# An attention and SiLU-MLP kernel: a hand-written interleaving exchanged for the order of a list scheduler, with chunked weight loads and 512-byte q and k rows

## The chip, the cores and the metric

One core of one Trainium2 chip runs the whole program. The metric is the device time of one execution in microseconds (us). Five engines work side by side and wait for one another by semaphores: TensorE (PE; its weight loads are listed apart as PEld), VectorE (DVE), ScalarE (ACT), GpSimd (POOL) and SyncE (SP), which here only issues transfers. Each engine executes its own list of instructions strictly in the order in which the program wrote it; an instruction that waits holds up everything behind it on that engine.

## The reference, cut to what matters

Inputs are q, k and v of shape (8 batches, 8 heads, 576 tokens, 64), w_in (512 x 2048) and w_out (2048 x 512), all float32. Per batch and head there are two attentions whose outputs are added:

```python
q_d, k_d, v_d = means over groups of 4 tokens          # 144 x 64 each
out_up    = repeat(softmax(q_d k_d^T / 8) v_d, 4)
mask      = |i - j| < 4
out_local = softmax(where(mask, q k^T / 8, -1e9)) v
x = out_up + out_local             # heads side by side: 4608 x 512
h = x @ w_in
out = (h * sigmoid(h)) @ w_out     # 4608 x 512, float32
```

## The kernel before, in words

**Pairs.** The 64 (batch, head) combinations are worked on as 32 pairs of heads; four pairs make one batch of 576 tokens. A pair p goes through these steps:

- `load(p)` on SP: q (`qs`) and k (`ks`) as [96, 12, 64] float32, that is rows of 64 elements (256 bytes); v twice, in five overlapping windows for each head (`vs`, two transfers, 256-byte rows) and in groups of four tokens (`vq`, 1024-byte rows). The staging tiles have two buffers each.
- `cast(p)` and `castv(p)` on POOL: q and k to bf16 (`qb`, `kb`), v to bf16 (`vb`), and the group sums of v (`vt`, `vd`).
- `ph_T`: TensorE transposes q and k (six 96-column blocks each) and forms their group means by a matmul with a small matrix `G_bf` of 24 columns. DVE copies the q results out of PSUM (`qT`, `qd`), ACT those of k (`kT`, `kd`).
- `ph_S1`, `ph_S2`: the scores of the band and of the small attention; ACT takes exp into `Pt` and `Pd`; DVE multiplies `Pt` by the band mask (`do_mask`).
- `ph_Z(z)`, once for two pairs 2z and 2z+1: row sums by matmuls with ones. ACT copies them to `zc`; then SP sends them through `zr` (40 x 72), DVE takes the reciprocal (`rr`, L387), SP writes it to a DRAM scratch `scr` and four transfers spread it over the partitions as `Rb` (L394).
- `ph_PV`: the products with v; DVE multiplies by `Rb` into `xo` (L417, L419), and `do_add` (L435) adds the small attention's part and writes the pair's 576 columns of `xT`, a ring of XR = 2048 token columns.

All these PSUM results share two double banks, `duo0` and `duo1`, taken in turn.

**MLP.** Tokens are handled in nine supers of 512. A `g1` tile is four matmuls into `hps` (contraction 512, weights `w_in_sb` in float32r), tanh on ACT (L453), and one DVE instruction (L455) that makes `gT`. A `g2` tile is four matmuls into `ops`; after four of them ACT copies the block to `osb` and SP writes it out. Each super has 16 g1 and 16 g2 tiles: 144 of each in all. Super j can start when all pairs of the batches that hold its tokens are in `xT`: `fill` demands 4 * min(j, 7) + 4 finished pairs.

**What sets the order.** `Prog.op` appends each operation to its engine's list and adds the semaphore waits that the data need. The order is that of the calls in the loop over `it`: T of pair it, two MLP tiles, Z, one tile, S1, two tiles, S2, two tiles, the reciprocal chain, PV of pair it - 3, two tiles. The list `mlp` alternates g1 of super j with g2 of super j - 1. Ahead of the loop two pairs are loaded, the constants (identity, `G_bf`, mask) are made on POOL between the first casts, and then POOL issues the loads of all of w_in (one transfer, 4096 KB) and all of w_out (one transfer, 2048 KB as bf16).

## Time and profile before

| | before |
|---|---|
| median of 3 runs (lowest to highest) | 485.42 us (484.01 to 486.57) |
| the profiled execution | 482.44 us |
| its span, first to last instruction | 480.7 us |
| mean granted TensorE clock | 0.954 of full speed |
| PE busy / DVE / ACT / POOL | 374.1 / 208.3 / 201.5 / 150.2 us |
| packets, of which under 512 B | 141718, 120946 |

How the rows further down are read. A row of the timeline has the start in us from the start of the span, the duration in us, the engine (SPq is the issue of a transfer on SP), the line, the operation with its output and inputs, and how many instructions were merged (x8); in square brackets stands how long the engine had been idle just before and what ended that. Two merged matmul groups can overlap on paper, so the price of a group is the distance from its start to the start of the next. A row of busy time by stretch has the stretch, its length, and for PE, PEld, DVE, ACT and POOL the busy us with the number of instructions; then the granted clock, the share of time that the core's transfer engines were busy, and GB/s. A row of a group of instructions has its mean duration in ns and the idle time before it.

### The profile page before, as it was taken

The numbers are of one execution on the slowest core, as the hardware profiler recorded it, in microseconds if no ns is written. First come the engines' busy times: TensorE is split into PE (matmuls) and PEld (weight loads), VectorE is DVE, ScalarE is ACT, GpSimd is POOL, SyncE is SP. The second block draws the span as 40 slices with busy tenths as digits, with TensorE's granted clock in tenths as the row PEclk, the third lists the DMA queues.
The fourth block names the chain that finished last, engine by engine and source line by source line (L and its number), as shares of the span: only waits on it lengthen the run. The fifth ranks groups of instructions, "written<-read, shape, count | busy, mean of one in ns | idle before, by whom it ended". The sixth has DMA issues, their size and how long they took to land.

```text
span 480.7 us, 7698 instructions
## 1 busy us (share of the span) xinstructions
PE 374.1 (78%) x3072; PEld 223.4 (46%) x3072; DVE 208.3 (43%) x361; ACT 201.5 (42%) x357; POOL 150.2 (31%) x187
## 2 busy tenths in 40 slices
PE   2311235299519997999899699979998979999997
PEld 1211223166306554555556365546554535555553
DVE  0210215157514564555666445655554554334320
ACT  3220224056405554556465345545654323444431
POOL 5922452632262424334352534244430000000000
PEclk9999999999658998999999979999998989999999
DMA  9999497692668695959689676969572031011012
GB/s 185 305 281 204 119 202 149 125 210 51 143 124 171 141 225 144 184 136 221 147 176 187 136 164 148 216 135 180 125 153 85 26 130 61 22 45 44 22 45 87
DMA packets 141718, 67.95 MB, mean 141 GB/s; under 512 B 120946, under 2 KB 132210, under 8 KB 141170
## 3 DMA queue, kind: packets, MB, share of 16 engines
q1 hardware_dynamic: 139090, 61.17, 58.7%
q0 software_dynamic: 2592, 6.29, 4.9%
q8 instruction: 24, 0.39, 0.4%
q14 instruction: 12, 0.10, 0.1%
HBM read 59.72 MB, written 9.63 MB: 144 GB/s over the span
## 4 chain that ended last, share of the span: by engine, by line
PE 65%; DMA 14%; SPq 7%; DVE 5%; POOL 4%; issue 3%; ACT 2%; POOLq 0%; ACTq 0%
PE hps L300 29%; PE ops L300 25%; PE duo L300 8%; DMA ks<-in_k_dram 5%; DMA zr<-zc 4%; SPq L381 4%; PE duo L310 3%; DMA vq<-in_v_dram 2%; DVE xT L435 2%; SPq L269 2%; DMA Rb<-scr 1%; DVE xo L417 1%; ACT th L453 1%; DMA scr<-rr 1%; POOL kb L278 1%
## 5 line engine op out<-in xcount | busy, mean ns | idle before, releaser
L300 PE MATMUL hps<-xT,w_in_sb 128*128 128x512 f32 x576 | 188.0, 448 | 37.3 <-DVE xT L435 32.6
L455 DVE SCALAR_TENSOR_TENSOR gT<-th,hps 128x512 bf16<-128x512 f32 x144 | 98.9, 687 | 149.0 <-ACT th L453 148.6
L300 PE MATMUL ops<-w_out_bf,gT 128*128 128x512 bf16 x576 | 151.2, 391 | 0.0
L453 ACT ACTIVATE th<-hps 128x512 f32<-128x512 f32 x144 | 86.0, 597 | 152.9 <-PE hps L300 152.7
L300 PEld LDWEIGHTS hps<-xT,w_in_sb 128*128 128x128 f32 x576 | 108.2, 198 | 74.7 <-DVE xT L435 36.2
L300 PEld LDWEIGHTS ops<-w_out_bf,gT 128*128 128x128 bf16 x576 | 46.7, 99 | 65.9 <-issue 26.1
L278 POOL CAST qb<-qs 96x768 bf16<-96x768 f32 x32 | 26.2, 820 | 126.4 <-DMA qs<-in_q_dram 103.0
L322 ACT ACTIVATE kT<-duo 128x576 bf16<-128x576 bf16 x32 | 20.8, 651 | 57.9 <-PE duo L300 57.9
L286 POOL TENSOR_TENSOR vt<-vq 72x512 f32<-72x512 f32 x32 | 41.1, 1286 | 6.8 <-DMA vq<-in_v_dram 6.6
L335 ACT ACTIVATE Pt<-duo 128x912 bf16<-128x912 f32 x32 | 29.7, 929 | 28.5 <-PE duo L300 28.5
L300 PE MATMUL duo<-qT,kT 64*128 64x112 bf16 (+1 forms) x320 | 20.0, 236 | 25.5 <-DVE qT L317 21.3
L284 POOL CAST vb<-vs 128x640 bf16<-128x640 f32 x32 | 24.0, 750 | 44.4 <-PE duo L300 28.7
L387 DVE RECIPROCAL rr<-zr 40x72 f32<-40x72 f32 x17 | 10.1, 593 | 62.5 <-DMA zr<-zc 62.5
L358 DVE TENSOR_TENSOR Pt<-Pt,mask_bf 128x1152 bf16<-128x1152 bf16 x32 | 25.5, 798 | 25.4 <-ACT Pt L350 18.5
L310 PE MATMUL duo<-id_bf,qb 96*128 96x96 bf16 x192 | 16.5, 233 | 25.5 <-POOL qb L278 25.5
L278 POOL CAST kb<-ks 96x768 bf16<-96x768 f32 x32 | 28.2, 882 | 25.3 <-DMA ks<-in_k_dram 24.7
L300 PEld LDWEIGHTS duo<-qT,kT 64*128 64x128 bf16 x320 | 11.1, 103 | 46.0 <-issue 36.0
L469 ACT ACTIVATE osb<-ops 128x512 f32<-128x512 f32 x36 | 21.5, 598 | 24.4 <-PE ops L300 23.8
L435 DVE TENSOR_TENSOR xT<-xo 128x576 fp32r<-128x576 f32 (+4 forms) x40 | 30.7, 783 | 0.6
L310 PEld LDWEIGHTS duo<-id_bf,qb 96*128 96x128 bf16 x192 | 12.1, 112 | 32.7 <-POOL qb L278 26.3
L288 POOL TENSOR_TENSOR vd<-vt 72x256 bf16<-72x256 f32 x32 | 24.5, 766 | 4.3
L417 DVE TENSOR_TENSOR xo<-duo,Rb 128x456 f32<-128x456 f32 x32 | 19.1, 596 | 7.4 <-DMA Rb<-scr 6.7
(43 smaller groups left out, 245.2 us busy)
## 6 DMA issues: line engine op xcount, KB each, us to landing
Rb<-scr SPq DMA_DIRECT2D x68, 180.0 KB, 3.6
vs<-in_v_dram SPq DMA_DIRECT2D x64, 160.0 KB, 4.7
...
```

The lines of the kernel that those rows point to most:

```text
L278: pool(lambda g, a=a, bb=bb: g.tensor_copy(bb[j][:, :, :, :], a[i][:, :, :].rearrange("p (h c) d -> p c h d", h=2)), r=[R(f"{nm}s{i}")], w ...
L284: pool(lambda g: g.tensor_copy(vb[m][:, :, :], vs[i][:, :, :]), r=[R(f"vs{i}")], w=[R(f"vb{m}")])
L286: pool(lambda g: g.tensor_tensor(vt[:, :, :], vq[i][:, :, 0:128], vq[i][:, :, 128:256], ALU.add), r=[R(f"vq{i}")], w=[R("vt")])
L288: pool(lambda g: g.tensor_tensor(vd[m][:, :, :], vt[:, :, 0:64], vt[:, :, 64:128], ALU.add), r=[R("vt")], w=[R(f"vd{m}")])
L300: return P.op("PE", lambda t: t.matmul(out_, lhsT, rhs, start=start, stop=stop, skip_group_check=True), r, w)
L310: P.op("PE", lambda t, c=c, st=st, tps=tps: t.transpose(tps[:, 96 * c:96 * c + 96], st[j][:, c, :, :].rearrange("p h d -> p (h d)"), id_bf ...
L335: P.op("ACT", lambda e: e.activation(Pt[m][:, :, 0:456], D[:, :, 0:456], AF.Exp, scale=0.125), r=bk, w=[R(f"P{m}")])
L358: P.op("DVE", lambda e: e.tensor_tensor(Pt[m][:, :, :], Pt[m][:, :, :], mask_bf[:, :].unsqueeze(1).to_broadcast([128, 2, S_]), ALU.mult), ...
L417: P.op("DVE", lambda e: e.tensor_tensor(xo[x][:, 0:456], D[:, 0, 0:456], Rb[u][:, 0:456], ALU.mult), r=[bk[0], R(f"Rb{u}")], w=[R(f"xo{x}")])
L435: P.op("DVE", lambda e, dst=dst, in0=in0, in1=in1: e.tensor_tensor(dst, in0, in1, ALU.add), r=[R(f"xo{x}")], w=xblk(kc, t, e_))
L453: P.op("ACT", lambda e: e.activation(th[tb][:, :], hps[hb][:, :], AF.Tanh, scale=0.5), r=[R(f"h{hb}", True)], w=[R(f"th{tb}")])
L455: P.op("DVE", lambda e: e.scalar_tensor_tensor(gT[j % 2][:, f, :], th[tb][:, :], 1.0, hps[hb][:, :], ALU.add, ALU.mult), r=[R(f"h{hb}", Tr ...
```

## The change

1. **Order.** The loop and `fill` go. Each step becomes a task with the tasks it needs, the tiles it reads and writes, and a check of the ring; `Prog` carries a clock for each engine and for the two transfer queues, fed by a table of costs in the code. At each step the scheduler issues whatever side work (loads, casts, masks, reciprocals, spreads of `Rb`) is due, then the attention task that its model says is ready (those of the same TensorE mode first, then PV, Z, S2, S1, T), else a g1 or g2 tile.
2. **Weights** come in eight transfers (`load_w`): w_in in four column chunks, w_out in four row chunks, each issued on POOL behind the loads of pairs 3 to 7.
3. **512-byte rows.** q and k are loaded as [96, 6, 128]: two neighbouring tokens in one row. The transposed blocks come out with even and odd tokens apart, so the copies `qT` (DVE) and `kT` (ACT) now write with a step of two elements; `G_bf` gets 48 columns and its matmuls accumulate in twos.
4. **Direct row sums for pairs 2 and 3** (`ph_ZD`, `do_recipD`): row sums on 64 columns of ones into the MLP's own banks `ops` and `hps`, and the reciprocal by DVE straight from there into `Rb`, in five pieces a pair, with no transfers.
5. **Smaller items.** The casts of q and k of the first four pairs move from POOL to DVE (q) and ACT (k); all constants are made before POOL's first cast of v; `Rb` has 4 buffers instead of 3; the ring `xT` has 1536 columns instead of 2048, and PV of a batch waits in the schedule until the supers that it overwrites have been read; the spread of `Rb` is a task of its own (`do_bcast`).

```diff
-        XR = 2048
+        XR = 1536
-        NST, NVB, NP_, NR = 2, 5, 5, 3
-        qs = sb("qs", [96, 12, 64], F32, NST)
+        NST, NVB, NP_, NR, NEARLY = 2, 5, 5, 4, 4
+        qs = sb("qs", [96, 6, 128], F32, NST)
...
+                    t[i][:, :, :], src[b, h:h + 2].rearrange("h (c p r) d -> p (h c) (r d)", p=96, r=2)),
...
+                src = tps[:, :].rearrange("p (c r g) -> p c r g", c=3, r=2)
+                dst = xt[j][:, :].rearrange("p (c g r) -> p c r g", c=3, r=2)
                 if nm == "q":
-                    P.op("DVE", lambda e, tps=tps: e.tensor_copy(qT[j][:, :], tps[:, :]),
+                    P.op("DVE", lambda e, src=src, dst=dst: e.tensor_copy(dst, src),
...
+        def load_w(c):
+            if c < 4:
+                P.op("POOL", lambda g: g.dma_start(
+                    w_in_sb[:, :, 512 * c:512 * c + 512],
...
-        P.op("POOL", lambda g: g.dma_start(w_in_sb[:, :, :], moe_w_in.rearrange("(kc p) f -> p kc f", p=128)),
-        for it in range(NPAIR + LAG):
-            if it < NPAIR:
-                ph_T(it)
...
+        wsteps = {3: (0, 1), 4: (2, 3), 5: (4,), 6: (5, 6), 7: (7,)}
+        before = {4: 'w1', 5: 'w3', 6: 'w4', 7: 'w6'}
...
+            task(attn, f"PV{p}", "PE", [f"rD{p}_4" if p in direct else f"b{z}", f"cv{p}"] +
+                 ([f"Z{z}"] if p not in direct else []) + [nm("PV", p - 1)],
+                 [R(f"P{m}"), R(f"Pd{m}"), R(f"vb{n}"), R(f"vd{n}"), R(f"Rb{u}")], duo_w,
+                 lambda p=p: ph_PV(p), "col", lambda p=p: ring_ok(p))
...
+            if ready:
+                ready.sort(key=lambda c: (c[2][6] != mode[0], c[1]))
...
+            elif mready:
+                if len(mready) == 2:
+                    want = "g2" if (last not in ("g1", "g2") or last == "g1") else "g1"
```

**Place 1: SP, around the first spread of `Rb`.** Before, from the loads of pair 4 on (`zr`, `scr` and `Rb` belong to pairs 0 and 1):

```order
L262 DMA qs<-in_q_dram 96x12x64
L262 DMA ks<-in_k_dram 96x12x64
L269 DMA vs<-in_v_dram 128x5x64 x2
L271 DMA vq<-in_v_dram 72x4x256
L381 DMA zr<-zc 10x1x72 x4
L388 DMA scr<-rr 40x72
L394 DMA Rb<-scr 64x720 x4
L262 DMA qs<-in_q_dram 96x12x64
```

Now, from the q load of pair 5 on, up to the same `Rb` (the `zr` transfers stand ahead of pair 4's loads):

```order
L291 DMA qs<-in_q_dram 96x6x128
L291 DMA ks<-in_k_dram 96x6x128
L445 DMA scr<-rr 40x72
L302 DMA vs<-in_v_dram 128x5x64 x2
L304 DMA vq<-in_v_dram 72x4x256
L291 DMA qs<-in_q_dram 96x6x128
L291 DMA ks<-in_k_dram 96x6x128
L302 DMA vs<-in_v_dram 128x5x64 x2
L304 DMA vq<-in_v_dram 72x4x256
L454 DMA Rb<-scr 64x720 x4
```

The first `Rb` stood behind the loads of five pairs and now stands behind those of seven.

**Place 2: PE, where a batch's last PV meets the next super.** Before, the end of pair 11, and the first g1 tile of super 2 right behind it:

```order
L300 MATMUL duo<-qT,kT 128x120 x2
L300 MATMUL duo<-qd,kd 72x144 x4
L300 MATMUL ops<-w_out_bf,gT 128x512 x4
L300 MATMUL duo<-Pt,vb 64x120 x2
L300 MATMUL duo<-Pt,vb 64x112 x6
L300 MATMUL duo<-Pt,vb 64x120 x2
L300 MATMUL duo<-Pd,vd 64x144 x4
L300 MATMUL hps<-xT,w_in_sb 128x512 x4
```

Now, the PV of pairs 18 and 19 (pair 19 is the last that super 4 needs):

```order
L347 MATMUL duo<-Pt,vb 64x120 x2
L347 MATMUL duo<-Pt,vb 64x112 x6
L347 MATMUL duo<-Pt,vb 64x120 x2
L347 MATMUL duo<-Pd,vd 64x144 x4
L347 MATMUL duo<-Pt,vb 64x120 x2
L347 MATMUL duo<-Pt,vb 64x112 x6
L347 MATMUL duo<-Pt,vb 64x120 x2
L347 MATMUL duo<-Pd,vd 64x144 x4
L347 MATMUL ops<-w_out_bf,gT 128x512 x4
L347 MATMUL hps<-xT,w_in_sb 128x512 x4
L347 MATMUL duo<-qT,kT 128x120 x2
```

Before, the tile behind PV is the 33rd g1 tile, the first of super 2, and so needs what this PV yields. Now 58 g1 tiles stand ahead of pair 19's PV, and super 4 begins with the 65th: six more come before its data are wanted. Counted in the same way for pairs 7, 11, 15, 19, 23, 27 and 31, before has 0, 0, 0, 0, 0, 0 and 9 tiles in hand, and now 0, 3, 4, 6, 12, 14 and 14.

## Rows read from the trace of the kernel before

**Rows 1.** Busy time by stretch, columns as told above.
```profile
24.00:36.00 12.00, 2.23 (x37) 1.30 (x35) 1.36 (x4) 3.21 (x6) 2.54 (x3) 1.00 1.15 282
0.00:95.00 95.00, 25.61 (x374) 19.46 (x374) 18.58 (x36) 21.36 (x39) 47.16 (x72) 1.00 0.93 198
95.00:150.00 55.00, 38.31 (x351) 25.44 (x352) 27.06 (x46) 23.78 (x43) 17.64 (x20) 0.78 0.70 140
150.00:400.00 250.00, 232.68 (x2005) 134.90 (x2004) 137.93 (x243) 127.42 (x228) 85.44 (x95) 0.96 0.68 151
```

**Rows 2.** The chain of waits, start, us and what, of 15 to 60 us.
```profile
19.17 25.05 DMA ks<-in_k_dram
```

**Rows 3.** The timeline of the first 61 us.
```profile
4.33 0.82 POOL L278 CAST qb<-qs 96x768 bf16<-96x768 f32 x1 [2.53 <-DMA qs<-in_q_dram]
5.83 0.82 POOL L278 CAST kb<-ks 96x768 bf16<-96x768 f32 x1 [0.67 <-DMA ks<-in_k_dram]
...
8.74 1.26 POOL L286 TENSOR_TENSOR vt<-vq 72x512 f32<-72x512 f32 x1 [0.45 <-DMA vq<-in_v_dram]
...
55.37 2.45 SPq L394 DMA_DIRECT2D Rb<-scr  x4
...
59.22 0.63 DVE L417 TENSOR_TENSOR xo<-duo,Rb 128x456 f32<-128x456 f32 x1 [2.15 <-DMA Rb<-scr]
...
60.22 0.76 DVE L435 TENSOR_TENSOR xT<-xo 128x576 fp32r<-128x576 f32 x1
```

**Rows 4.** The timeline of PE where the MLP begins.
```profile
94.76 0.79 PE L300 MATMUL hps<-xT,w_in_sb 128*128 128x512 f32 x1 [9.33 <-DVE xT L435]
...
96.70 3.76 PE L300 MATMUL hps<-xT,w_in_sb 128*128 128x512 f32 x8
```

**Rows 5.** Who waited for whom: us in total, times, longest.
```profile
PE hps L300 <- DVE xT L435: 32.6, 7, 9.8
```

**Rows 6.** The timeline of PE, 199 to 230 us, attention and MLP mixed.
```profile
199.62 0.43 PE L310 MATMUL duo<-id_bf,qb 96*128 96x96 bf16 x6
...
200.44 1.02 PE L300 MATMUL ops<-w_out_bf,gT 128*128 128x512 bf16 x4
...
202.33 0.43 PE L300 MATMUL duo<-Pt,ones_bf 128*32 128x360 bf16 x8
...
202.81 1.04 PE L300 MATMUL ops<-w_out_bf,gT 128*128 128x512 bf16 x4
203.78 0.37 PE L300 MATMUL duo<-qT,kT 64*128 64x120 bf16 x8
204.09 1.19 PE L300 MATMUL hps<-xT,w_in_sb 128*128 128x512 f32 x4
...
206.10 0.23 PE L300 MATMUL duo<-qT,kT 64*128 64x120 bf16 x2
...
206.38 1.21 PE L300 MATMUL hps<-xT,w_in_sb 128*128 128x512 f32 x4
...
208.40 0.44 PE L300 MATMUL duo<-Pt,vb 128*64 128x120 bf16 x10
...
208.90 1.20 PE L300 MATMUL hps<-xT,w_in_sb 128*128 128x512 f32 x4
...
229.03 0.96 PE L300 MATMUL hps<-xT,w_in_sb 128*128 128x512 f32 x3
```

**Rows 7.** The timeline of the last 22 us, MLP alone.
```profile
459.05 1.04 PE L300 MATMUL ops<-w_out_bf,gT 128*128 128x512 bf16 x4
...
460.86 1.04 PE L300 MATMUL ops<-w_out_bf,gT 128*128 128x512 bf16 x4
...
477.61 0.60 ACT L469 ACTIVATE osb<-ops 128x512 f32<-128x512 f32 x1 [2.86 <-PE ops L300]
```

**Rows 8.** Groups of instructions: busy us, mean ns, idle before and releaser.
```profile
L317 DVE COPY qT<-duo 128x576 bf16<-128x576 bf16 x32 | 14.3, 447 | 10.9 <-PE duo L300 10.9
L387 DVE RECIPROCAL rr<-zr 40x72 f32<-40x72 f32 x17 | 10.1, 593 | 62.5 <-DMA zr<-zc 62.5
```

More of the change, by code (lines that the diff above doesn't have):

```diff
@@ L46 @@
     ENGS = ("PE", "ACT", "DVE", "POOL", "SP")
+    LATENCY = {"PE": 200, "ACT": 100, "DVE": 100, "POOL": 120, "SP": 50}
     def __init__(self):
@@ L51, in __init__, with ready @@
         self.dcount = {}
+        self.free = {e: 0 for e in self.ENGS}
+        self.ring = {"SP": 0, "POOL": 0}
+    def ready(self, eng, r, w):
+        t = 0
+        for x in r:
+            for o in (x.last.values() if x.psum else x.writers):
+                if o.eng != eng or o.dsem:
+                    t = max(t, o.end + self.LATENCY[o.eng])
+        for x in w:
+            for o in (x.last.values() if x.psum else x.readers or x.prev):
+                if o.eng != eng or o.dsem:
+                    t = max(t, o.end + self.LATENCY[o.eng])
+        return t
     def _dep(self, op, d, know, forced):
@@ L88, in op @@
         deps = [(d, f) for d, f in deps if d is not op]
+        t = self.free[eng]
+        for d, f in deps:
+            if d.eng != eng or d.dsem:
+                t = max(t, d.end + self.LATENCY[d.eng])
+        if dma:
+            other = self.ring["POOL" if eng == "SP" else "SP"]
+            self.free[eng] = max(t + 600, self.ring[eng] - 4000)
+            begin = max(self.free[eng], self.ring[eng])
+            self.ring[eng] = begin + cost + min(cost, max(0, other - begin)) // 2
+            op.end = self.ring[eng] + 1800
+        else:
+            self.free[eng] = op.end = t + cost
         deps.sort(key=lambda df: -(df[0].pos if not df[0].dsem else 1 << 30))
@@ L401, in ph_PV @@
             m, n, u, x = p % NP_, p % NVB, p % NR, p % 2
-            b, kc = divmod(p, 4)
-            def pv(c):
+            for c in range(5):
                 for h in range(2):
@@ L408, in pv @@
                     mm(o, vb[n][:, 5 * h + c, :], Pt[m][:, h, QB[c]:QB[c] + NQ[c]],
-                       [R(f"P{m}"), R(f"vb{n}")], [bk[0] if c < 4 else bk[1]])
-            for c in range(5):
-                pv(c)
+                       [R(f"P{m}"), R(f"vb{n}")], [bk[0] if c < 4 else bk[1]], cost=27, m="col")
             for s in range(2):
@@ new lines, in bass_hourglass_attn__then__act_silu_kernel, with ring_ok, duo_w, task @@
+        NT_PAIR = NPAIR
+        done, g1n, g2n = set(), [0], [0]
+        direct = (2, 3)
+        def ring_ok(p):
+            b = p // 4
+            lo = (b + 1) * S_ - XR
+            return lo <= 0 or g1n[0] >= 16 * ((lo + 511) // 512)
+        def duo_w():
+            return [R(f"duo{nph[0] % 2}a", True), R(f"duo{nph[0] % 2}b", True)]
+        side, attn = [], []
+        def task(lst, name, eng, pre, r, w, fn, m="full", ok=None):
+            lst.append((name, eng, [x for x in pre if x], r, w, fn, m, ok))
@@ new lines, in z_of, with rank, when, run_side @@
+        def z_of(p):
+            return f"d{p}"
+        def rank(name):
+            return [name.startswith(x) for x in ("PV", "Z", "S2", "S1", "T")].index(True)
+        def when(t):
+            name, eng, pre, r, w, fn, m, ok = t
+            if any(x not in done for x in pre) or (ok and not ok()):
+                return None
+            return P.ready(eng, r, w() if callable(w) else w)
+        def run_side(now, horizon):
+            nxt, again = None, True
+            while again:
+                again, nxt = False, None
+                for t in side[:90]:
+                    tm = when(t)
+                    if tm is None:
+                        continue
+                    tm = max(tm, P.free[t[1]] - 1000)
+                    if tm <= now + horizon:
+                        side.remove(t)
+                        done.add(t[0])
+                        t[5]()
+                        log.append((now, t[0]))
+                        again = True
+                        break
+                    nxt = tm if nxt is None else min(nxt, tm)
+            return nxt
@@ new lines, in run_mlp @@
+        def run_mlp(kind):
+            if kind == "g1":
+                j, f = divmod(g1n[0], 16)
+                g1n[0] += 1
+                g1(j, f)
+            else:
+                j, i = divmod(g2n[0], 16)
+                g2n[0] += 1
+                g2(j, i)
+        const_id()
+        now, last, log = 0, "", []
+        load_qk(0)
+        done.add("lqk0")
+        side = [t for t in side if t[0] != "lqk0"]
+        const_g()
+        done.add("G")
+        const_mask()
+        done.add("mask")
```

363 lines of the change are left out of this document (232 added, 131 removed).

## The prediction

> **What bounds the kernel now.** I read the busy time by stretch first: 95 us at the start in which TensorE works 25.6 us while the transfer engines are 93% taken, then stretches in which TensorE is nearly full [rows 1]. So there are two limits in turn: transfers until the MLP has input, TensorE afterwards. Then the chain of waits, to see what is late in the first part: one k load of pair 3 is on the chain for 25.05 us, beside both weight loads [rows 2]. The timeline shows what follows from it: `Rb` of pair 0 ends its wait only at 59.22 [rows 3], and the first g1 tile is complete at 94.76, after 9.33 us in which TensorE waited for `xT` [rows 4]. Last, the table of waits: TensorE waited 32.6 us for L435 in seven places [rows 5]. These are the super boundaries, where the order puts the PV of the last pair directly ahead of the tile that needs it; DVE's multiply and add, and the spread of `Rb` before them, lie bare there.
>
> What TensorE needs at full speed comes from the dense rows. MLP alone: one g1 and one g2 tile every 460.86 - 459.05 = 1.81 us [rows 7]; 144 of them are 260.6 us. Attention, start to next start [rows 6]: T 0.82, Z 0.48, S1 0.31, S2 0.28, PV 0.50. The stretch from 199.62 to 229.03 is 29.41 us and holds 11 g1 and 12 g2 tiles (20.8 us), three each of T, S1, S2 and PV and two Z (6.7 us); the 1.9 us left over, on 14 attention blocks between MLP tiles, make 0.14 us for each such change.
>
> From the first g1 tile to the end the order of both kernels still holds 25 T, 25 S1 and S2, 28 PV and 13 Z: 20.5 + 14.8 + 14.0 + 6.2 = 55.5 us. Before, with 107 blocks: 260.6 + 55.5 + 15.0 + 3.1 (from the last `osb` copy's start, 477.61, to 480.7 [rows 7]) = 334.2 us. It took 480.7 - 94.8 = 385.9. The 52 us between are waits (16.7 us idle in the stretch to 150, 17.3 in that to 400) and low clock, granted 0.78 in the one and 0.96 in the other [rows 1].
>
> **The change part by part.** *The start.* All of it hangs on when `Rb` of pairs 0 and 1 lands, since pairs 2 and 3 no longer use that way. One q or k load took 5.83 - 4.33 = 1.50 us, the three v loads of a pair 8.74 - 5.83 = 2.91 [rows 3]. For the 512-byte rows no row exists. If the time goes by bytes, q or k stays at 1.50; if by rows, it falls to 0.75; I take 1.20, nearer to the former, because v's loads, with 1024-byte rows in nearly half of their bytes, moved 623 KB in 2.91 us, 214 KB per us, against 295 KB in 1.50, 197. A pair then costs 2 x 1.20 + 2.91 = 5.3 us (4.4 to 5.9). Weights: 6.29 MB at the 282 GB/s of 24 to 36 us [rows 1] are 22.3 us; 5.77 MB, seven of the eight chunks, are issued ahead of pair 0's `Rb` and cost 20.4. `Rb` itself took 59.22 - 55.37 = 3.8 us [rows 3]. The first place of the order shows that it now waits behind seven pairs: 1.5 + 7 x 5.3 + 20.4 + 3.8 = 62.8 us, later than the 59.22 of before. What is gained comes behind it: pairs 0 to 3 follow without a second round through `zr`, `scr` and `Rb`. DVE needs from one `xo` to the end of the add about 1.78 us (59.22 to 60.22, plus 0.76 [rows 3]), four times, and one mask lies between: 8 us. First g1 tile at 70.8, against 94.76.
>
> The ten direct reciprocals of 152 or 132 columns cost DVE between 0.59 us, the price of 72 columns, and 0.59 x 152 / 72 = 1.25 each [rows 8], at most 12.5 us in all, and lie in the time until 62.8, when DVE has little else; without that cover the first g1 tile is later by what sticks out. The casts that move from POOL to DVE and ACT (0.82 us each [rows 3]) take some 3.3 us from each in the same stretch and free POOL for constants and v. Constants ahead of the first `castv` delay v and not q or k, and v is wanted only at PV. All of these I put at nothing.
>
> *The step of two in `qT`.* DVE's copy takes 447 ns now [rows 8]; stepped writes cost between nothing and a doubling, 0.45 us a pair. I take nothing: from 150 to 400 us DVE is busy 138 of 250 us [rows 1], and TensorE has MLP tiles between T and S1. The cover is missing where S1 directly follows T, in the first pairs, which wait for transfers anyway. The Trainium skill speaks against this edit: "VectorE: DVE Perf Modes", section "What auto-detection actually checks", lets the two-elements-a-cycle mode start only where every tensor is 16-bit with step 1. By it DVE gets up to 32 x 0.45 = 14 us more work, which this sum still puts under the MLP tiles.
>
> *The second super.* It needs pairs 4 to 7. On the transfer side, ahead of their last `Rb`, the order has the q and k loads of 16 pairs, the v loads of 13, all weights and three spreads: 1.5 + 16 x 2.4 + 13 x 2.91 + 22.3 + 2 x 2.4 + 3.8 = 108.6, and two rounds of DVE, 3.6, make 112. On TensorE, from 70.8 on: 16 g1 and 12 g2 tiles at 0.905, 25.3; 7 T, 5.5 S1 and S2, 4 PV, 2 Z, 11.9; 14 blocks, 2.0; and slow clock at the start, where eight matmuls took 3.76 instead of 1.81 us [rows 4], 2.0. That is 112.0 as well. The two limits meet, so slower transfers would show at once, and faster ones would bring nothing here.
>
> *From there.* The second place of the order shows six tiles in hand at super 4; with 3 to 14 in hand from super 2 on, the waits for L435 should go, and I keep 3 us of stalls (0 to 17, the idle time from 150 to 400). Changes between attention and MLP fall from 107 to 69: 9.7 us. The smaller ring does not bind the other way: 46 g1 and 59 g2 tiles follow the last PV, so attention ends some 95 us ahead of the end.
>
> *The chunked weights* run on POOL's queue beside SP's loads. That k took 25.05 us beside them [rows 2] shows that the two share the engines, so I add their times. The Trainium skill says the same ("DMA: Bandwidth & Descriptors", section "Issuing engines are not separate DMA queues"); the trace agrees.
>
> *Sum.* 70.8 + 260.6 + 55.5 + 9.7 + 2.0 + 3.1 + 3 = 404.7 us of span, say 405; around it lie 482.44 - 480.7 = 1.7 us: 407 us. The median of the runs before is 3.0 us above the profiled execution, which I leave in the range.
>
> **The rivals.** *A. The start is not serial.* Weight chunks 5 to 7 fall behind `Rb` (5.6 us less), or q and k go by rows (7 x 0.9 = 6.3 us less), and no stalls remain: 390 to 398, say 394. For it: two queues; against it: transfers were 93% busy to 95 us [rows 1].
>
> *B. 512-byte rows bring nothing.* q and k stay at 1.50 each: the second super then waits until 1.5 + 48 + 37.8 + 22.3 + 8.6 + 3.6 = 122, 10 us late: 417. For it: 197 and 214 KB per us are close together. Against it: the rows are really halved in number.
>
> *C. The stalls stay in another form.* A fixed order made from estimates meets transfers that vary; SP, in order, holds `Rb` back behind loads that wait for a buffer. At the idle rate of 150 to 400 us, 17.3 in 250, the 290 us after 112 lose 20 us instead of 3, and a granted clock of 0.96 some 10 more: 424 to 434. Against it: three or more tiles in hand from super 2 on.
>
> *D. Slower than before: the queue on SP becomes the bound.* After the first g1 tile 14 couples of pairs must pass through `zr`, `scr` and `Rb`, each behind two or three pairs' loads, and these behind POOL's casts. Before the last 95 us there are 480.7 - 70.8 - 95 = 315 us for them: the change loses from 22.5 us a couple on. At 24 us it ends at 70.8 + 336 + 95 = 502, 504 with what lies around. For it: two loaded pairs and one spread now stand ahead of each other in one queue that can't overtake. Against it: at the start, with nothing else to do, two couples took 94.76 - 59.22 = 35.5 us, 17.8 each, weights no longer in the way [rows 3, 4].
>
> **How the numbers follow.** Forecast 0.44, A 0.18, B 0.15, C 0.18, D 0.05. About 0.5% is what a measurement of this kernel can tell from no change. Faster takes all but D and a sliver for an unforeseen loss: 0.94; of the rest 0.02 falls within 0.5% and 0.04 is slower. The range begins at 388, below A, and ends at 433, where C ends; D and the ends of A and C lie outside.
>
> **What would show it.** First complete g1 tile at 71 us (64 to 75), the first of the second super at 112 (105 to 122), and the last PV about 95 us before the end. The wait of `hps` for L435 falls from 32.6 to under 8 us. Packets fall by 36864, half of q's and k's 73728 rows of 256 bytes, to some 105 thousand. `qT` tells of the step: 447 to 894 ns. The start is wrong if `Rb` of pair 0 lands far from 62.8; the claim on tiles in hand is wrong if TensorE waits for `xT` or `Rb` past 150 us; and the forecast falls if TensorE is idle for more than 20 us between 112 us and the end.

## The result, and the profile after

| | before | after |
|---|---|---|
| median (lowest to highest), 4 runs each | 484.72 us (483.90 to 486.57) | 421.27 us (420.16 to 425.20) |
| ratio, 95% interval | | 0.870 [0.864, 0.875] |
| the profiled execution, its span | 482.44, 480.7 | 425.2, 423.5 |
| granted TensorE clock, mean | 0.954 | 0.98 |
| PE / DVE / ACT / POOL busy, us | 374.1 / 208.3 / 201.5 / 150.2 | 355.2 / 243.5 / 205.2 / 155.2 |

The change is worth 63 us. The forecast was 407 us, with 388 to 433 around it: sign and range hold, the time is 14 us above. The profiled execution is the longest of its runs; others had a clock of 0.987 to 0.996 and spans of 418.4 to 419.8 us. Where some executions of a kernel fell into a slower state (one of 1884 us is the most extreme), the medians and ranges given from here on leave them out.

Busy time by stretch, the kernel after; the first four rows answer to [rows 1], the next is the stretch from the first g1 tile to the second super's, and four shorter ones follow:

```profile
24.00:36.00 12.00, 3.19 (x46) 2.45 (x42) 5.30 (x7) 2.88 (x6) 2.73 (x4) 1.00 1.25 341
0.00:95.00 95.00, 41.84 (x533) 31.83 (x535) 47.70 (x66) 36.24 (x64) 50.66 (x74) 1.00 1.08 223
95.00:150.00 55.00, 51.29 (x518) 33.32 (x523) 40.08 (x62) 32.29 (x58) 31.96 (x34) 0.94 1.00 217
150.00:400.00 250.00, 242.29 (x1898) 150.48 (x1927) 152.28 (x242) 130.66 (x229) 72.56 (x77) 0.98 0.50 128
...
78.90:125.10 46.20, 43.48 (x443) 29.25 (x446) 30.65 (x49) 28.03 (x52) 23.97 (x25) 0.93 0.95 203
...
60.00:95.00 35.00, 22.15 (x253) 15.83 (x251) 24.16 (x32) 15.96 (x31) 19.46 (x21) 1.00 0.95 191
76.00:82.00 6.00, 4.45 (x48) 3.10 (x37) 3.49 (x5) 3.09 (x5) 4.32 (x5) 1.00 0.35 90
95.00:115.00 20.00, 17.61 (x176) 12.07 (x177) 14.29 (x22) 10.92 (x20) 13.25 (x14) 0.83 1.02 210
150.00:200.00 50.00, 46.79 (x440) 29.21 (x445) 34.72 (x55) 27.15 (x48) 24.12 (x27) 0.90 0.80 192
```

The transfer engines are now full for most of the time up to 150 us (1.08 and 1.00 of the time, 0.93 and 0.70 before; the share is the sum of the packets' times and can exceed 1): the loads that were spread over the run are drawn to its front. TensorE works 41.8 of the first 95 us instead of 25.6, and idles 7.7 us in the 250 from 150 on instead of 17.3.

Who waited for whom on PE, after 65 us (us in total, times, longest):

```profile
PE duo L347 <- DVE xo L498: 14.9, 6, 6.3
...
PE hps L347 <- DVE gT L542: 1.5, 2, 1.0
```

The wait of `hps` for `xT`, 32.6 us in [rows 5], is gone altogether. What is left is the wait of PV for the multiply that empties the bank before it (`xo`); of its 14.9 us only 1.7 lie behind 150 us.

The timeline: the casts of q and k of pair 0 (now on DVE and ACT), then from the landing of the first `Rb` to the first g1 tile (DVE, POOL and PE rows in order of time), and the first tile of the second super; to be held against [rows 3, 4]:

```profile
4.51 0.56 DVE L315 CAST qb<-qs 96x768 bf16<-96x768 f32 x1 [4.51 <-DMA qs<-in_q_dram]
...
5.55 0.84 ACT L318 ACTIVATE kb<-ks 96x768 bf16<-96x768 f32 x1 [3.46 <-DMA ks<-in_k_dram]
...
64.79 0.63 DVE L498 TENSOR_TENSOR xo<-duo,Rb 128x456 f32<-128x456 f32 x1 [8.55 <-DMA Rb<-scr]
65.80 0.76 DVE L517 TENSOR_TENSOR xT<-xo 128x576 fp32r<-128x576 f32 x1
67.98 1.68 DVE L517 TENSOR_TENSOR xT<-xo 128x576 fp32r<-128x576 f32 x1
69.19 1.05 POOL L330 TENSOR_TENSOR vd<-vt 72x256 bf16<-72x256 f32 x1
69.58 5.14 DVE L412 TENSOR_TENSOR Pt<-Pt,mask_bf 128x1152 bf16<-128x1152 bf16 x1
70.97 0.84 POOL L321 CAST qb<-qs 96x768 bf16<-96x768 f32 x1
...
73.28 0.82 POOL L321 CAST kb<-ks 96x768 bf16<-96x768 f32 x1
75.64 1.52 DVE L517 TENSOR_TENSOR xT<-xo 128x576 fp32r<-128x576 f32 x1
78.07 1.11 DVE L517 TENSOR_TENSOR xT<-xo 128x576 fp32r<-128x576 f32 x1
78.92 2.07 PE L347 MATMUL hps<-xT,w_in_sb 128*128 128x512 f32 x4
...
125.11 2.22 PE L347 MATMUL hps<-xT,w_in_sb 128*128 128x512 f32 x8
```

`Rb` of pair 0 ends its wait at 64.79, 2.0 us behind the forecast. Then DVE needs 14.1 us instead of 8.0: one mask takes 5.14 us, beside four casts that POOL runs back to back (the first and the last are shown), and two adds take twice the 0.76 of the first.

Groups of instructions that answer to [rows 8], with `kT`'s copy, the mask and the plain add:

```profile
L375 ACT ACTIVATE kT<-duo 128x576 bf16<-128x576 bf16 x32 | 26.3, 821 | 39.8 <-PE duo L347 39.7
L370 DVE COPY qT<-duo 128x576 bf16<-128x576 bf16 x32 | 25.5, 796 | 12.0 <-PE duo L347 11.8
L412 DVE TENSOR_TENSOR Pt<-Pt,mask_bf 128x1152 bf16<-128x1152 bf16 x32 | 32.1, 1006 | 6.9 <-ACT Pt L404 6.9
L517 DVE TENSOR_TENSOR xT<-xo 128x576 fp32r<-128x576 f32 x24 | 28.2, 1174 | 0.8
```

and `kT`'s copy, mask and add before, which were not shown:

```profile
L322 ACT ACTIVATE kT<-duo 128x576 bf16<-128x576 bf16 x32 | 20.8, 651 | 57.9 <-PE duo L300 57.9
L358 DVE TENSOR_TENSOR Pt<-Pt,mask_bf 128x1152 bf16<-128x1152 bf16 x32 | 25.5, 798 | 25.4 <-ACT Pt L350 18.5 <-POOL mask_bf L255 7.0
L435 DVE TENSOR_TENSOR xT<-xo 128x576 fp32r<-128x576 f32 x24 | 22.7, 945 | 0.5
```

`qT` went from 447 to 796 ns. Mask and add, whose instructions are unchanged, went from 798 to 1006 and from 945 to 1174 ns. The packets, from the page:

```profile
DMA packets 105665, 66.43 MB, mean 157 GB/s; under 512 B 47006, under 2 KB 95134, under 8 KB 105630
```

141718 less 105665 is 36053; the predicted 36864 were the rows of q and k.

**Where the 57 us between the two profiled executions went.** The kernel after was profiled a second time, beside later experiments (span 422.1). Busy time by stretch, to 125 us and behind it, the kernel before:

```profile
0.00:125.00 125.00, 50.77 (x594) 36.15 (x596) 37.68 (x67) 38.39 (x70) 56.24 (x82) 1.00 0.85 179
125.00:480.60 355.60, 323.34 (x2480) 187.24 (x2480) 170.66 (x294) 163.07 (x288) 94.00 (x105) 0.94 0.56 128
```

and the second profile of the kernel after:

```profile
0.00:125.00 125.00, 69.41 (x784) 48.30 (x785) 65.93 (x96) 50.36 (x89) 70.57 (x94) 0.99 1.03 219
125.00:422.00 297.00, 288.81 (x2290) 176.67 (x2287) 174.78 (x278) 153.99 (x271) 84.04 (x92) 0.99 0.52 131
```

TensorE idles 125 - 50.8 = 74.2 us of the first stretch before and 55.6 after, and 32.4 and 8.3 us behind it; its own work falls from 374.1 to 358.2 us, at a clock of 0.954 and 0.987. So of 58.6 us some 19 are a fuller start, 24 are waits later on, and 16 are the clock and denser work.

The same numbers for every kernel of this study, with the spans. Super 1 and super 2 are here the first and the second super (the kernel's own count begins at 0); the columns give the start of tanh on the first tile of each, 1 to 2 us behind the start of the tile's matmuls. A star marks traces in which 38 to 40 of 3072 matmul records are missing, which, judged by the two profiles of after, makes about 3 us less busy and 4 more idle.

| kernel | span | PE busy | idle to 125 us | idle after | super 1 | super 2 |
|---|---|---|---|---|---|---|
| before | 480.7 | 374.1 | 74.2 | 32.4 | 95.59 | 144.28 |
| after* | 423.5 | 355.2 | 55.7 | 12.6 | 81.03 | 126.57 |
| after, profiled again | 422.1 | 358.2 | 55.6 | 8.3 | 80.24 | 127.77 |
| order alone | 442.7 | 358.1 | 69.2 | 15.4 | 93.27 | 132.55 |
| before with 512-byte rows* | 476.1 | 369.7 | 73.8 | 32.6 | 95.54 | 144.74 |
| after with 256-byte rows | 433.5 | 358.2 | 60.2 | 15.1 | 81.21 | 133.50 |
| after with whole weights | 416.9 | 357.6 | 50.3 | 9.0 | 74.22 | 124.37 |
| after without direct sums | 426.4 | 359.8 | 53.8 | 12.8 | 79.35 | 123.74 |
| tiny casts* | 420.4 | 353.7 | 55.0 | 11.7 | 74.55 | 127.76 |
| casts on ACT* | 422.9 | 353.4 | 54.2 | 15.3 | 74.97 | 126.99 |
| small v loads | 409.9 | 351.9 | 49.9 | 8.1 | 71.82 | 117.23 |
| four direct pairs* | 416.7 | 354.3 | 49.7 | 12.7 | 81.88 | 115.08 |
| four direct pairs, whole weights | 413.2 | 355.9 | 48.1 | 9.2 | 76.78 | 111.75 |
| four direct pairs, casts on ACT | 417.2 | 355.4 | 54.3 | 7.5 | 87.00 | 115.64 |

### The profile page after: what moved, and what is told of

The parts are those of the page before. It is cut to its first block, busy times and chain, and to the rows that moved or that the text cites. A ratio compares the mean times of both kernels' runs of the same rounds, so it can differ in the third digit from the quotient of the medians.

```text
span 423.5 us, 7628 instructions
## 1 busy us (share of the span) xinstructions
PE 355.2 (84%) x3033; PEld 225.3 (53%) x3072; DVE 243.5 (58%) x373; ACT 205.2 (48%) x360; POOL 155.2 (37%) x185
## 2 busy tenths in 40 slices
DMA packets 105665, 66.43 MB, mean 157 GB/s; under 512 B 47006, under 2 KB 95134, under 8 KB 105630
## 4 chain that ended last, share of the span: by engine, by line
PE 64%; DMA 14%; DVE 9%; SPq 4%; issue 4%; POOL 2%; ACT 2%; POOLq 0%; ACTq 0%
PE hps L347 27%; PE ops L347 26%; PE duo L347 8%; DMA vq<-in_v_dram 7%; DMA Rb<-scr 5%; PE duo L359 3%; DVE xT L517 3%; DVE Pt L412 2%; DVE xo L498 2%; SPq L291 2%; DMA scr<-rr 1%; DVE xo L500 1%; SPq L302 1%; POOL vt L328 1%; DVE gT L542 1%
## 5 line engine op out<-in xcount | busy, mean ns | idle before, releaser
L347 PE MATMUL hps<-xT,w_in_sb 128*128 128x512 f32 x576 | 182.3, 442 | 1.7 <-DVE gT L542 1.5
L347 PE MATMUL ops<-w_out_bf,gT 128*128 128x512 bf16 x537 | 139.0, 382 | 4.4 <-issue 3.3
L326 POOL CAST vb<-vs 128x640 bf16<-128x640 f32 x32 | 24.5, 767 | 66.6 <-PE duo L347 58.6
L375 ACT ACTIVATE kT<-duo 128x576 bf16<-128x576 bf16 x32 | 26.3, 821 | 39.8 <-PE duo L347 39.7
L328 POOL TENSOR_TENSOR vt<-vq 72x512 f32<-72x512 f32 x32 | 43.2, 1349 | 6.2 <-DMA vq<-in_v_dram 6.2
L321 POOL CAST qb<-qs 96x768 bf16<-96x768 f32 x28 | 23.7, 847 | 52.6 <-PE duo L347 34.4
L517 DVE TENSOR_TENSOR xT<-xo 128x576 fp32r<-128x576 f32 (+2 forms) x40 | 39.2, 996 | 1.1
L359 PE MATMUL duo<-id_bf,qb 96*128 96x96 bf16 x192 | 16.7, 235 | 26.4 <-POOL qb L321 18.3
L412 DVE TENSOR_TENSOR Pt<-Pt,mask_bf 128x1152 bf16<-128x1152 bf16 x32 | 32.1, 1006 | 6.9 <-ACT Pt L404 6.9
L330 POOL TENSOR_TENSOR vd<-vt 72x256 bf16<-72x256 f32 x32 | 31.2, 974 | 4.3
L370 DVE COPY qT<-duo 128x576 bf16<-128x576 bf16 x32 | 25.5, 796 | 12.0 <-PE duo L347 11.8
L359 PEld LDWEIGHTS duo<-id_bf,qb 96*128 96x128 bf16 x192 | 11.7, 113 | 34.4 <-POOL qb L321 18.9
L347 PEld LDWEIGHTS duo<-qT,kT 64*128 64x128 bf16 x320 | 12.2, 102 | 27.2 <-DVE xo L498 11.7
L321 POOL CAST kb<-ks 96x768 bf16<-96x768 f32 x28 | 23.6, 842 | 7.0 <-DMA ks<-in_k_dram 7.0
```

Of the source, the lines that this page charges most:

```text
L321: pool(lambda g, d=dst, s=src: g.tensor_copy(d, s), r=[R(f"{nm}s{i}")], w=[R(f"{nm}b{j}")], cost=830)
L328: pool(lambda g: g.tensor_tensor(vt[:, :, :], vq[i][:, :, 0:128], vq[i][:, :, 128:256], ALU.add), r=[R(f"vq{i}")], w=[R("vt")], cost=1290)
L330: pool(lambda g: g.tensor_tensor(vd[m][:, :, :], vt[:, :, 0:64], vt[:, :, 64:128], ALU.add), r=[R("vt")], w=[R(f"vd{m}")], cost=750)
L347: return P.op("PE", lambda t: t.matmul(out_, lhsT, rhs, start=start, stop=stop, skip_group_check=True), r, w, cost=cost)
L359: P.op("PE", lambda t, c=c, r=r, w=w, tps=tps: t.transpose(tps[:, 192 * c + 96 * r:192 * c + 96 * r + 96], w, id_bf[:, :]), r=[R("id"), R( ...
L375: P.op("ACT", lambda e, src=src, dst=dst: e.activation(dst, src, AF.Copy), r=[bk[x]], w=[R(f"kT{j}")], cost=650)
```

## The experiments

### The parts of the change, one at a time

**Order alone** (256-byte rows, two whole weight transfers behind pair 1, no direct sums, all casts on POOL; the scheduler stays, and with it the constants ahead of the first cast of v, the four `Rb` buffers and the smaller ring).

```diff
-        NST, NVB, NP_, NR, NEARLY = 2, 5, 5, 4, 4
+        NST, NVB, NP_, NR, NEARLY = 2, 5, 5, 4, 0
...
-        direct = (2, 3)
+        direct = ()
...
-        wsteps = {3: (0, 1), 4: (2, 3), 5: (4,), 6: (5, 6), 7: (7,)}
+        wsteps = {1: (0, 4)}
...
```

> The scheduler alone: 256-byte rows, weights in two whole transfers behind pair 1, no direct row sums, casts of the first pairs on POOL; what stays of the change is the order, the constants ahead of the first cast of v, a ring of 1536 columns and four Rb buffers. Theory (tiles in hand are worth some 40 us from the first g1 tile on, whatever the start): first g1 tile 90 to 105 us, from there 340 to 350 us, total 433 to 452. Rival (the order gains only because transfers got shorter): from the first g1 tile on 365 us or more, total 460 or more.

Measured: 441.26 us, ratio 0.912 [0.905, 0.918]. The order alone brings some 43 of the 63 us. Its waits on PE:

```profile
PE duo L358 <- POOL qb L320: 34.2, 7, 10.9
PE duo L346 <- DVE xo L497: 21.3, 8, 8.0
...
PE hps L346 <- DVE gT L541: 5.9, 6, 2.1
```

`hps` no longer waits for `xT` here either, so it is the order, with the small items that stayed in, that removes the boundary waits. Most of its gain lies behind 125 us: 17 us less idle there, and over the whole span 16 us less busy, at a clock of 0.988 in the mean. Up to 125 us 69.2 us are idle, 5 less than before, and super 1 comes only 2.3 us earlier. The fuller start is the work of the other parts. Which of them is open: of the runs below that take one part out, none makes super 1 more than 1 us later than in the second profile of after. The casts of the first four pairs, moved to DVE and ACT, were not tried alone; with all casts on POOL, TensorE waited 46 us for POOL's casts up to 95 us here, against 23 in the kernel after, and the first `xo` stood at 75.77 instead of 64.79.

**512-byte rows alone, put into the kernel before** (order of before unchanged).

```diff
-        qs = sb("qs", [96, 12, 64], F32, NST)
+        qs = sb("qs", [96, 6, 128], F32, NST)
...
-                    P.op("DVE", lambda e, tps=tps: e.tensor_copy(qT[j][:, :], tps[:, :]),
+                    P.op("DVE", lambda e, src=src, dst=dst: e.tensor_copy(dst, src),
...
```

> The kernel before with the 512-byte rows alone (staging, casts, group means in twos, stepped copies). Theory (its waits are at the super boundaries and in the chain of row sums, not in the sum of transfers): 472 to 483, a part of it at the start. Rival 1 (the rows carry the change): 465 or less. Rival 2 (the stepped copies, 0.35 us more on DVE and 0.17 on ACT for each pair, lie on the path): 485 or more.

Measured: 479.87 us, ratio 0.989 [0.982, 0.996]: a gain of 5 us. Super 1 does not move (95.54). Its largest wait on PE, in total, is the old one:

```profile
PE hps L300 <- DVE xT L437: 29.1, 7, 9.5
```

**256-byte rows in the kernel after** (order of after unchanged).

```diff
-        qs = sb("qs", [96, 6, 128], F32, NST)
+        qs = sb("qs", [96, 12, 64], F32, NST)
...
-                    t[i][:, :, :], src[b, h:h + 2].rearrange("h (c p r) d -> p (h c) (r d)", p=96, r=2)),
+                    t[i][:, :, :], src[b, h:h + 2].rearrange("h (c p) d -> p (h c) d", p=96)),
...
```

> The changed kernel with q and k in rows of 256 bytes again (staging, casts, group means, copies as before); the order of every engine stays that of the changed kernel (421.3 us). Theory (transfers bound the start): in the changed kernel k landed 1.04 us behind q, before it was 1.50 us, so pair 0's Rb comes about 7 x 2 x 0.46 = 6.4 us later and the second super up to 10 us: 427 to 433 us, with nearly all of the loss ahead of the second super; qT back to about 0.45 us. Rival 1 (the short rows carried most of the 63 us): 445 us or more, with loss in every stretch. Rival 2 (the rows are nothing, the copies cost what they gave): 419 to 423.

Measured: 435.25 us, ratio 0.897 [0.888, 0.906], 11 to 14 us slower than the two medians of after (421.27, and 423.82 below). It is dearer than expected, and dearer than in the old order, though `qT` is back at 447 ns:

```profile
L369 DVE COPY qT<-duo 128x576 bf16<-128x576 bf16 x32 | 14.3, 447 | 11.9 <-PE duo L346 11.8
```

So the stepped copies' 11 us more of DVE time, 32 times 0.35, are well paid. Super 1 hardly moves; super 2 comes 5.7 to 6.9 us later, and beside the second profile of after TensorE idles 4.6 us more up to 125 us and 6.8 behind it. Its first k cast, and DVE's wait ahead of super 2, from the timeline:

```profile
4.57 0.56 DVE L314 CAST qb<-qs 96x768 bf16<-96x768 f32 x1 [4.57 <-DMA qs<-in_q_dram]
...
5.91 0.84 ACT L317 ACTIVATE kb<-ks 96x768 bf16<-96x768 f32 x1 [3.81 <-DMA ks<-in_k_dram]
...
125.95 0.63 DVE L497 TENSOR_TENSOR xo<-duo,Rb 128x456 f32<-128x456 f32 x1 [7.94 <-DMA Rb<-scr]
```

That `Rb` ends its wait at 125.95; in the kernel after, the same multiply stands at 120.11 and waited for PE in the first profile, and at 120.44 and waited 6.89 us for `Rb` in the second. So the two limits lie about a microsecond apart there. Rows of 512 bytes pay where transfers are the limit, and the new order has made them that up to 150 us; what the 6.8 us of idle time behind 125 us wait for was not followed up.

**Two whole weight transfers behind pair 1.**

```diff
...
-        wsteps = {3: (0, 1), 4: (2, 3), 5: (4,), 6: (5, 6), 7: (7,)}
-        before = {4: 'w1', 5: 'w3', 6: 'w4', 7: 'w6'}
+        wsteps = {1: (0, 4)}
+        before = {}
```

> The changed kernel with the weights in two whole transfers, issued behind pair 1's v loads instead of eight chunks behind pairs 3 to 7; the scheduler orders the rest anew. Theory (the sum of all transfers ahead of pair 0's Rb decides, not their order): first g1 tile within 8 us of 78.9, total 419 to 430. Rival (the chunks keep the inputs from standing behind the weights, and that is what moved the start): first g1 tile 95 us or later, total 437 or more.

Measured: 418.83 us, ratio 0.864 [0.856, 0.871]. Chunking brings nothing; the interval touches that of after, so a small loss by it is possible and not settled. The scheduler orders TensorE's and DVE's work anew for it, and no mask meets four casts here: the first `xo` at 63.52, the first g1 tile at

```profile
71.60 2.59 PE L347 MATMUL hps<-xT,w_in_sb 128*128 128x512 f32 x4
```

8.1 us later, against the 8.0 of the prediction.

**No direct row sums.**

```diff
-        direct = (2, 3)
+        direct = ()
```

> The changed kernel without the direct row sums of pairs 2 and 3, which go through zc, zr, scr and Rb like all others; the scheduler orders the rest anew. Theory (the second round through DRAM is what the start was rid of): first g1 tile 12 to 18 us later than 78.9, total 432 to 440. Rival (a good order hides that round behind loads that have to come anyway): first g1 tile within 4 us, total 419 to 425.

Measured: 428.16 us, ratio 0.883 [0.878, 0.889]. My expectation was wrong: super 1 is not later but 1 to 2 us earlier, and TensorE idles no longer up to 125 us. The direct sums save 4 to 7 us of the median, all the same, and by the table that lies behind 125 us (12.8 us idle against 8.3). Which wait it is there I did not settle. From the first `xo` (61.99) to the first g1 tile (77.26) it takes 15.3 us although pairs 2 and 3 go the long way here, 15.5 with the order alone, and 35.5 before (59.22 to 94.76): it is the order, and not the direct sums, that made this stretch short.

### DVE beside POOL, and what an earlier start is worth

**Tiny casts.** POOL's casts of q and k of pairs 7 and 8, the four beside the long mask, copy 2 columns instead of 768; these two pairs work on older data, so this kernel leaves their own q and k out. The order is that of after.

```diff
+                elif p in (7, 8):
+                    pool(lambda g, d=bb[j], s=a[i]: g.tensor_copy(d[:, 0, 0, 0:2], s[:, 0, 0:2]),
```

> The changed kernel, same order on every engine, but POOL's four casts of q and k of pairs 7 and 8 copy two columns instead of 768 (those pairs' scores are left out of the computation in effect). They ran while one band mask of DVE, usually 0.7 to 0.8 us, took 5.14 us ahead of the first g1 tile. Theory (DVE was held up by POOL's run of casts, and the start misses its forecast by that): the mask there takes 0.7 to 1.4 us, the first tanh comes 4 to 6 us before 81.0; the end moves by 0 to 5 us, 416 to 421, since the second super also waits for transfers. Rival (the long mask waits for something else): it stays above 3 us, first tanh within 1 us.

Measured: 418.53 us, ratio 0.864 [0.857, 0.871]. The timeline, DVE, POOL and PE:

```profile
66.12 1.68 DVE L520 TENSOR_TENSOR xT<-xo 128x576 fp32r<-128x576 f32 x1
67.72 1.27 DVE L415 TENSOR_TENSOR Pt<-Pt,mask_bf 128x1152 bf16<-128x1152 bf16 x1
69.11 0.20 POOL L321 CAST qb<-qs 96x2 bf16<-96x2 f32 x1
...
72.44 2.07 PE L350 MATMUL hps<-xT,w_in_sb 128*128 128x512 f32 x4
...
120.14 0.63 DVE L501 TENSOR_TENSOR xo<-duo,Rb 128x456 f32<-128x456 f32 x1 [7.97 <-DMA Rb<-scr]
...
126.31 2.12 PE L350 MATMUL hps<-xT,w_in_sb 128*128 128x512 f32 x8
```

The mask falls from 5.14 to 1.27 us, and the first g1 tile follows its `Rb` by 9.5 us instead of 14.1. So the casts do hold DVE up, by 4.6 us; the tile comes 6.5 us earlier in all, since `Rb` too came 1.9 us earlier in this run. But super 2 stays where it was, now because DVE waits 7.97 us for `Rb`, and TensorE's idle time up to 125 us is what it was (55.0 and 55.7): the earlier start is lost again. The median is 3 to 5 us below those of after, with intervals that touch.

The Trainium skill ("SBUF — State Buffer", section "Who interferes with whom") says that a DVE instruction with two SBUF inputs, as the mask is, contends with a GpSimd instruction that reads SBUF, for a port pair that only one of the two can hold. The trace agrees that DVE is held up. It shows more than one instruction's worth, and the engine that began first was the one that lost: the mask, begun 1.39 us ahead of the first of the four casts, ended only 0.62 us behind the last one's end, while each cast kept its usual 0.82 to 0.84 us. For 0.66 of the 1.39 us POOL's `vd` was still running (to 70.24); why the mask was not done in the rest, as it was with the tiny casts, no run here shows.

**The same casts on ACT** (pairs 4 to 9).

```diff
+                elif p < 10:
+                    P.op("ACT", lambda e, d=dst, s=src: e.activation(d, s, AF.Copy),
...
```

> The changed kernel with the casts of q and k of pairs 4 to 9 on ACT instead of POOL; the scheduler orders anew. Theory (POOL's casts hold DVE up at the start, and ACT has room there): first tanh 3 to 6 us earlier than 81.0, total 414 to 420. Rival (ACT's exps come later for it): first tanh later, total 422 to 428.

Measured: 425.81 us, ratio 0.879 [0.872, 0.885]. Super 1 comes 6 us earlier (74.97), the mask takes 1.27 us again, super 2 is not earlier (126.99), TensorE's idle time up to 125 us is 54.2, and nothing of the gain is left at the end. Two ways of freeing DVE agree that a start of super 1 some 6 us earlier does not bring super 2 forward. That transfers alone take the gain is shown by neither: here ACT also carries twelve more casts (busy 214.6 us instead of 205.2), and the time is the one that the rival gave for that.

### What sets the time up to the second super

**Small v loads.** The order of after; the v loads of pairs 4 to 7 move 8 partitions, so this kernel leaves most of their v out.

```diff
+                n = 8 if 4 <= p < 8 else 128
...
-                P.op("SP", lambda s, win=win, hh=hh: s.dma_start(vs[i][:, 5 * hh:5 * hh + 5, :], win),
+                P.op("SP", lambda s, win=win, hh=hh, n=n: s.dma_start(vs[i][0:n, 5 * hh:5 * hh + 5, :], win),
...
```

> The changed kernel with the same order on every engine, but the v loads of pairs 4 to 7 move 8 partitions instead of 128 and 72, so that these pairs work on older v: nearly four times 2.91 us of transfer (11.6 us) are left out of the time before the second super, three of them ahead of the first Rb. Theory (transfers set the time until both supers can start): first xo at 56 us instead of 64.79, first g1 at 68 to 71 instead of 78.92, first g1 of the second super at 111 to 117 instead of 125.1, and the whole 409 to 414 us against 421.3. Rival (TensorE and the attention's own work set the second super, as they did when only the casts were shortened: 418.5 us with the first tanh 6.5 us earlier): second super at 122 to 127, the whole 418 to 422.

Measured: 413.40 us (411.65 to 414.99), ratio 0.858 [0.852, 0.864], beside 423.82 for the kernel after in the same comparison: 10 us less. The timeline:

```profile
55.36 0.61 DVE L503 TENSOR_TENSOR xo<-duo,Rb 128x456 f32<-128x456 f32 x1
60.38 5.13 DVE L417 TENSOR_TENSOR Pt<-Pt,mask_bf 128x1152 bf16<-128x1152 bf16 x1
...
69.71 2.07 PE L352 MATMUL hps<-xT,w_in_sb 128*128 128x512 f32 x4
...
111.21 0.63 DVE L503 TENSOR_TENSOR xo<-duo,Rb 128x456 f32<-128x456 f32 x1 [7.41 <-DMA Rb<-scr]
...
115.77 2.12 PE L352 MATMUL hps<-xT,w_in_sb 128*128 128x512 f32 x8
```

Both starts move with the transfer time left out: the first `xo` comes 9.4 us earlier, the first g1 tile 9.2, super 2's first tile 9.3. The long mask is still there (5.13). The second profile of after has 5.7 us more idle time up to 125 us and 6.3 us more of busy time, at a clock of 0.987 in the mean against 1.000 here, so a part of the 10 us is the clock. Of the edits that leave after's order as it is, this one alone brought super 2 forward, and it gave the largest gain.

**Four direct pairs** (pairs 0 to 3 instead of 2 and 3): no spread of `Rb` for the first super at all.

```diff
-        direct = (2, 3)
+        direct = (0, 1, 2, 3)
...
```

The row sums of pairs 2 and 3 also wait for the reciprocals of the pair two before.

> The changed kernel with direct row sums for pairs 0 and 1 too, so that no pair of the first super waits for Rb through DRAM; the scheduler orders anew. Theory (pair 0's Rb behind the loads of seven pairs sets the first g1 tile): first tanh 8 to 18 us before 81.0, but the second super stays with the transfers, so the end gains less: 413 to 420. Rival (DVE, with ten more reciprocals of 1 us, becomes the late one): first tanh within 4 us of 81.0 or later, total 420 to 426.

Measured: 416.66 us, ratio 0.858 [0.849, 0.867], clear of the second comparison of after (0.875 [0.871, 0.878]) but not of the first ([0.864, 0.875]). Super 1 gains nothing (81.88), because PE waits 6.8 us for POOL's casts ahead of it; super 2 comes 12 us earlier. TensorE idles 6 us less up to 125 us, and that is the gain: in another order the mark of super 2 says little, since MLP tiles that come earlier only change places with attention work.

**Four direct pairs with whole weights**, both edits as above.

> Direct row sums for pairs 0 to 3 and the two whole weight transfers behind pair 1, both in one kernel. Theory (chunked weights bring nothing, and the spreads of Rb taken out of SP's queue bring the second super forward): first g1 of the second super at 110 to 116 as with direct sums for four pairs alone, the whole 412 to 416 us. Rival (the two gains of 2.4 and 4.6 us are one and the same wait, or noise): 417 to 422.

Measured: 417.29 us (415.56 to 420.29), ratio 0.861 [0.857, 0.864]; the kernel after beside it had 0.875 [0.871, 0.878]. Its interval lies below that of after beside it and just reaches that of the first comparison; between this version and four direct pairs alone nothing can be told apart. Super 2's first tile stands at 110.53, within the theory's 110 to 116, but the time is that of the rival. The gain is again idle time up to 125 us, 48.1 instead of 55.6 us; behind it nothing changes (9.2 and 8.3). The two gains don't add up, and super 2 was the wrong mark to read them by.

**Four direct pairs with the casts on ACT.**

> Direct row sums for pairs 0 to 3, and the casts of q and k of pairs 4 to 9 on ScalarE instead of GpSimd. Theory (DVE's long masks and adds beside GpSimd's casts cost the first start 6 us, and four direct pairs keep the gain because the second super is no longer late): first tanh at 75 to 78 instead of 81.9, second super at 108 to 114, the whole 410 to 415 us. Rival (ScalarE pays for the casts later, as with the casts alone: 425.8 against 421.3): 418 to 426.

Measured: 418.00 us, ratio 0.862 [0.857, 0.866], the time of the rival. The theory failed at its first number: super 1 begins at 87.00, not at 75 to 78. PE waits for exp, which in ACT's order now stands behind casts that wait for q and k (the row is after 65 us):

```profile
PE duo L362 <- ACT Pt L392: 2.7, 1, 2.7
```

**The kernel after once more**, beside the last three.

> The changed kernel once more, beside the three others on the same chip: 419 to 424 us if the first comparison stands, and the yardstick for differences of a few us between the variants.

Measured: 423.82 us, ratio 0.875 [0.871, 0.878]. Differences of 3 us between comparisons are within what two of them vary by.

## Why the prediction was right, and where it fell short

By its own terms the profiled execution's 18.5 us above the 405 divide so:

| term | forecast | measured | more |
|---|---|---|---|
| first `xo` | 62.8 | 64.79 | 2.0 |
| from there to the first g1 tile | 8.0 | 14.1 | 6.1 |
| to the second super's first tile | 41.2 | 46.2 | 5.0 |
| to the end | 293 | 298.4 | 5.4 |

All four terms came out late, so none made up for another. The two marks on the way, 78.9 and 125.1, lie outside the ranges that the prediction gave them (64 to 75, 105 to 122); that the whole stayed inside 388 to 433 is owed to the width of that range.

- **The boundary waits** went as predicted, from 32.6 us to none, and with the order alone; past 150 us TensorE never waits for `xT`, and 1.7 us for `xo`. TensorE's idle time after 125 us is 8.3 us in the complete trace (10.4 from 112 us), more than the 3 kept for stalls and under the 20 at which the forecast was to fall.
- **The start up to `Rb`** held to 2 us: seven pairs and seven of the eight weight chunks do lie ahead of it. Within the sum it is partly luck: the first `xo` came 9.4 us behind the issue of `Rb` (55.36) instead of 3.8, and `Rb` was issued 3.6 us sooner than the sum has it. The ten direct reciprocals took 0.9 to 1.1 us each and began between 24 and 50 us, under the cover named (five of them in the tile's view below).
- **What the direct sums were to bring** failed as a reason, though not as a number. The prediction put the gain of the start down to pairs 2 and 3 without a second round. Without direct sums super 1 came no later, and from the first `xo` to the first g1 tile it took 15.3 us against 14.1 with them: the order had already cut the 35.5 us of before.
- **The 8 us of DVE** failed as a price: the durations of adds and mask were taken from a stretch in which POOL left DVE alone. With the casts made tiny it is 9.5 us, with whole weights 8.1.
- **The second super, 112,** is the term that decides, and it came 13 us later (125.1). The prediction had two limits meet there, and they do, only later. On TensorE's side the start is 8.1 us later, and 5.0 more follow. The clock (0.93 in that stretch) costs 0.07 x 46.2 = 3.2, only 1.2 more than the 2.0 that the sum had kept for it; the other 3.8 are open. On the side of the transfers the last `Rb` was forecast to land at 108.6; with tiny casts, where nothing else holds DVE, it ended its wait at 120.14, and with small v loads, 11.6 us of transfers less, at 111.21. This is the step that failed: a pair's loads were priced at 1213 KB in 5.3 us, 229 GB/s, and without a break, while the core moved 191 GB/s from 60 to 95 us and 210 from 95 to 115. The bytes are those of the forecast, 26.4 MB up to 120 us; the time for them is not. Two things are in it. One is a pause: from 76 to 82 us the core moved 90 GB/s, its engines 0.35 taken, because SP, which issues in order, stood waiting for ACT's copy of the row sums ahead of `zr` and issued no load from 71.4 to 80.2 us (SP's waits, up to 95 us):

```profile
SPq L437 <- ACT zc L433: 5.7, 1, 5.7
```

At 229 GB/s it is worth (229 - 90) x 6 / 229 = 3.6 us, an estimate. The other is a lower rate: tiny casts and whole weights have no such pause there, and with their engines 1.08 and 1.07 taken the core still moved only 204 and 211 GB/s from 60 to 95 us. I carried the price of the first, quiet loads into a stretch where `zr`, `scr` and `Rb` pass too. That it is these small transfers that lower the rate was not tried by itself, and how much of the 11.5 us (120.1 against 108.6) each of the two causes is not settled: with tiny casts a later pause, 49 GB/s from 97.5 to 100.5 us, takes the place of the first.
- **From there to the end** 293 was right in size: with small v loads, the order that of after and the clock 1.00 from there on, it is 409.9 - 115.8 = 294.1. In the profiled execution of after TensorE was granted 0.90 from 150 to 200 us, which is 5 us; what drew it down was not tried.
- **The step of two in `qT`** cost 0.35 us a copy, short of the doubling, and its cover held. The Trainium skill ("VectorE: DVE Perf Modes", section "What auto-detection actually checks"), as the prediction read it, made that up to 14 us of DVE time; it is 11.2, and 512-byte rows won 11 to 14 us net all the same.
- **The 512-byte rows.** The first k cast follows the first q cast by 5.55 - 4.51 = 1.04 us, against 5.91 - 4.57 = 1.34 with 256-byte rows in the same order: between the bounds 0.75 and 1.50, with my 1.20 not far off.
- **Rivals.** B gave 417 and a second super at 122, nearer to the numbers than the forecast, and is refuted as a cause: without the rows it is 435.3. A fell, as the start is serial (small v loads move it one for one). C is partly true: 8 to 13 us of stalls, not 20, some 5 of its 10 us of clock, and SP's order does hold transfers back, though ahead of the second super. D fell: the last `xo` starts at 326.4, 97 us before the end against the 95 forecast, as the view of the tile `Rb` shows (ns shortest, median, longest; first and last start):

```profile
L498 DVE TENSOR_TENSOR xo<-duo,Rb x32: 558/625/633, 64.8 to 326.4; 128x456 f32<-128x456 f32 x32
L481 DVE RECIPROCAL Rb<-ops x5: 911/1035/1108, 24.4 to 40.4; 128x152 f32<-128x152 f32 x3, 128x132 f32<-128x132 f32 x2
```
